# Packed attention and two MoE layers on one core: the first pass of the seven-product layer reordered

## The chip, the cores and the metric

The kernel runs on one core of a Trainium2 chip. TensorE (PE) multiplies, VectorE (DVE), ScalarE (ACT) and GpSimd (POOL) do elementwise work, and SyncE (SP) issues all DMAs of this kernel. Each engine takes its instructions strictly in the order in which they were written, and so does SP's queue: a DMA whose data is not ready holds up every DMA behind it. The metric is the device time of one execution in microseconds (us), the median of several runs.

## The reference, cut to what matters

All arrays are float32 or float64 bits; tokens are 8 batches x 576 = 4608 rows.

```python
p_packed = sm_attn(p, k, v)             # 64 heads, 32 packed rows each
x = sm_attn(q, p_packed, p_packed)      # -> (4608, 512)
h = x @ w_in                            # 512 x 1024
solu = h * softmax(h)
x = layernorm(solu) * g_ln @ w_out      # 1024 x 512
h = x @ moe2_w_in                       # 512 x 2048
g = maximum(h, 0) ** 2
return g @ moe2_w_out                   # 2048 x 512
```

The weights arrive as float64; the kernel reads them as pairs of int32 words and decodes them to float32 itself.

## The kernel before, in words

**Order of the work.** The kernel does not write its instructions directly. It hands operations to a planner (class `Plan`) with an engine, an estimated duration, an urgency (a planned time in us) and the tiles that they read and write. The planner simulates five engines that always take the most urgent operation that is ready, and then writes all instructions in the order that it found. So constants such as `DZ = 6.913` (planned us for one group of the first pass) and the urgency of an operation decide the order on each engine, and nothing else: on the chip only the order and the data count.

**Precision.** Every float32 operand is split into a high part and a rest. `mm` (L389) makes three matmuls of each product: high x high (L396), high x rest (L397), rest x high (L398).

**Stages.** Up to about 536 us the kernel computes attention and the first MoE layer (with POOL's help). Then come two passes for the last two products of the reference, each done with a seven-product scheme on 2 x 2 blocks in place of eight block products.

**First pass** (`z_group`, 536 to 914 us, "z"): `h = x @ moe2_w_in` and `g`. Six blocks of 768 tokens, each with 8 groups. A group has seven products 1, 2, 6, 5, 7, 3, 4 of six matmuls (128 x 128 weights `zi`, 384 columns of `y`), that is 2016 matmuls in all. Products 1, 6, 7 and 4 of a group add up in one bank `px`, one after the other; product 2 goes to `pw`, products 5 and 3 to `pz`. After products 1, 6 and 7 ACT copies the sum so far out of `px` (L928, `snap`), and the next product on `px` must wait for this copy. After product 4 ACT takes the relu (L962). DVE adds `pw` or `pz` to a copy (L932), and DVE (L937) or ACT (L940, L941) takes relu and square of the sum (`finish`). Each result is stored to `g_dram` by a DMA. The copies live in a ring of 11 `gw` slots.

**Weights of the second pass.** While blocks 1 to 4 of the first pass run, 16 calls of `prepare` fetch `moe2_w_out` as raw words (four DMAs of 128 KB into one tile `w2raw`, which the profile shows as `w2raw<-in_moe_w_out_dram` and the order of instructions as `w2raw<-in_moe2_w_out_dram`), decode them (first ACT's absolute value L411, then DVE L414 to L430, whose L430 is the last to read the raw tile), form the seven combinations and store them to `o_dram`. There is one slot for the raw words, `wo20`.

**Second pass** (`o_products`, 914 to 1286 us, "o"): `g @ moe2_w_out`. Six blocks of 768 tokens, seven products 4, 1, 5, 6, 2, 7, 3, each of 8 steps j of nine matmuls (three token tiles, 256 columns), 3024 matmuls in all. Each step needs a 384-column piece `ga` of `g_dram`, split by ACT (L378) and DVE (L381, both write `cb`), and DVE makes sums of pieces (L885). The weights `oi` of a product take over slots of the first pass: those of product 1 two slots of `y` loads (`v01`, `v11`), those of product 4 the four slots of `zi2`. Results are added up in `osb` (L1050, copies L1054) and stored to the output (`store`, L991), four DMAs of 32 rows for each tile of 128 tokens.

Of the kernel before, what the change touches and what calls it, by code (L numbers as in the profile page):

```python
# [245 lines left out]
def kernel(  # L246
# [25 lines left out]
    nc = tc.nc  # L272
# [21 lines left out]
    YB, ZL, OL, GL0, GL1, GL2, PS, CS = 138.73, 119.42, 25.08, 15.29, 10.0, 16.72, -26.16, 142.32  # L294
# [69 lines left out]
    def dma(at, out_, in_, nbytes, r=(), w=()):  # L364
        plan.op(DMA, max(430.0, nbytes / 358.0), at, lambda: nc.sync.dma_start(out=out_(), in_=in_()), r=r, w=w, lag=2200)  # L365
# [406 lines left out]
    def prepare(at, w_bits, rows2, cols2, outs, marks, tiles, r=(), engines=BOTH):  # L772

        raw, x, hi = tiles
        for i, (n, m) in enumerate(((0, 0), (0, 1), (1, 1), (1, 0))):
            dma(at, lambda i=i: raw()[:, i * P:(i + 1) * P], lambda n=n, m=m: w_bits[rows2[n]:rows2[n] + P, 2 * cols2[m]:2 * (cols2[m] + P)].rearrange(
                "p (f w) -> p f w", w=2), P * P * 8, r=list(r), w=[raw])
        decode(at, raw, 4 * P, x, part=lambda t: t[:, :4].rearrange("p b f -> p (b f)"), add=engines)
# [16 lines left out]
    T0, DT = 96.13, 17.76  # L795
    PD0, PD = 168.95, 30.084
    UD, UA, U1 = 32.796, 191.99, -65.87
    WI, WO, WOD, YL = 161.4, 266.68, 57.239, 3.29
# [22 lines left out]
    def weights_z():  # L821
        for k in range(16):
            c, n = divmod(k, 8)
            tiles = [m1.tile([P, 4 * P, 2], I32, "w2raw"), m1.tile([P, 7, P], F32, "wx"),
                     m1.tile([P, 7, P], F32R, "wh", tag="w2raw")]
            prepare(PD0 + PD * k, w2_in_bits, (c * P, (c + 2) * P), (n * P, F2 // 2 + n * P),
                    [lambda k=k, s=s: z_dram[s][:, :, k].rearrange("q p f -> p q f") for s in range(2)], [z_mark], tiles, [under_way])
# [4 lines left out]
    DZ, DO = 6.913, 8.163  # L832
# [24 lines left out]
    def load_o(at, p):  # L857
        def load(t, s, j, w):
            dma(at, lambda: t().bitcast(F32), lambda: o_dram[s][PLACE[p]][:, j:j + w], P * w * 2 * P * 4, r=[o_mark], w=[t])
        if p == 1:  # L860
# [4 lines left out]
        else:  # L865
            q = {7: 1, 4: 2, 5: 6, 6: 5, 2: 7, 3: 3}[p]
# [45 lines left out]

    def z_group(at, st, n):
        bx, bw, bz = pso.tile([P, 512], F32, "px", bufs=4), bank("pw"), bank("pz")
        y = ys[st]

        def product(p, ps, first):
            ts, view = zi[p]

# [4 lines left out]
            plan.op(PE, c_mm(6, HN), at, f, r=ts + y[p], w=[ps])  # L924

        def snap(ps):
            t = gw()
            plan.op(ACT, c_act(HN), at, lambda: nc.scalar.copy(t(), ps()[:, :HN]), r=[ps], w=[t])  # L928
            return t

        def add(t, ps):
            plan.op(DVE, c_dve(HN), at, lambda: nc.vector.tensor_tensor(t(), ps()[:, :HN], t(), op=ALU.add), r=[t, ps], w=[t])  # L932

        def finish(t, b, relu=True):
# [27 lines left out]
        plan.op(ACT, c_act(HN), at, lambda: nc.scalar.activation(c21(), bx()[:, :HN], AF.Relu), r=[bx], w=[c21])  # L962
        finish(c21, 2, False)
# [35 lines left out]
    def o_products(at, st):  # L999
# [13 lines left out]
        x = None  # L1013
        for k, p in enumerate(O_ORDER):
# [5 lines left out]
            for j in range(8):  # L1020
# [3 lines left out]
                if cbs[0] % 6 == 5:  # L1024
# [14 lines left out]
                def f(j=j, ch=ch, cl=cl, acc=acc, wv=wv, first=p not in (6, 7)):  # L1039
                    for i in range(NI):  # L1040
# [36 lines left out]
    def second():  # L1077
# [3 lines left out]
        for st in range(NSZ):  # L1081
            for n in range(8):
                z_group(T1 + DZ * (8 * st + n), st, n)
                k = 8 * st + n - 8
                if 0 <= k < 32 and k % 2 == 0:
                    j, q = divmod(k // 2, 2)
                    tiles = [wo_v.tile([P, 4 * P, 2], I32, "w2raw", tag="wo20"), wo_v.tile([P, 7, P], F32, "wx", tag="wo21"),
                             wo_v.tile([P, 7, P], F32R, "wh", tag="wo30")]
                    prepare(T1 + DZ * (k + 8) + PS, w2_out_bits, (j * P, (j + 8) * P), (q * P, 2 * P + q * P),
                            [lambda j=j, q=q, s=s: o_dram[s][:, :, j, q * P:(q + 1) * P].rearrange("q p f -> p q f") for s in range(2)], [o_mark], tiles, engines=(DVE,))  # L1090
# [41 lines left out]
```

## Time and profile before

| | |
|---|---|
| runs | 1296.13 us median of 3 (1293.94 to 1297.68) |
| the profiled execution | 1294.89 us, its span 1293.1 us |
| mean granted TensorE clock | 0.983 |
| PE matmuls busy | 1228.0 us (95% of the span) |
| PE weight loads busy | 1132.8 us (88%) |
| DVE busy | 945.4 us (73%) |
| ACT busy | 812.0 us (63%) |
| POOL busy | 258.1 us (20%) |

Busy times are sums over the span of one profiled execution; the span runs from the first to the last instruction. PE is shown in two rows, matmuls and weight loads, which overlap. An idle time is put down to what released the instruction behind it. In the rows further down, `L411` is line 411 of the kernel before, `a<-b` says that tile a is written from tile b, and `x17` counts instructions.

### The profile page before, as it was taken

How to read it: one execution, taken by the hardware profiler on the slowest of the kernel's cores; microseconds unless marked ns; L12 is line 12 of the kernel's file. 1: busy time of each engine (PE TensorE's matmuls, PEld its weight loads, DVE VectorE, ACT ScalarE, POOL GpSimd, SP SyncE). 2: the span in 40 equal slices, each digit the busy share in tenths (PEclk: the TensorE clock that was granted, in tenths of full speed). 3: DMA queues.
4: the chain of work that ended last, by engine and by line, in shares of the span. 5: the costliest groups of instructions: out<-in, count | busy, mean ns of one | idle time of the engine just before them, and what ended most of it. 6: DMA issues, size and time to landing. Idle time of an engine off the chain costs nothing.

```text
span 1293.1 us, 23520 instructions
## 1 busy us (share of the span) xinstructions
PE 1228.0 (95%) x8420; PEld 1132.8 (88%) x8420; DVE 945.4 (73%) x1844; ACT 812.0 (63%) x1699; POOL 258.1 (20%) x266
## 2 busy tenths in 40 slices
PE   5878999999999999999999999999899999999997
PEld 3436888887988889999999999999799999999997
DVE  6897888788778865448575868552678797878885
ACT  5666778677777776558676767685455554545452
POOL 2565554456545542000000000000000000000000
PEclk9887999999999999999999999999899999999999
DMA  7652462545354335985657576643985444443501
GB/s 247 207 143 82 124 182 77 154 126 140 107 147 142 102 103 196 324 284 195 212 173 257 167 257 195 213 179 114 362 327 189 124 141 141 124 150 96 176 22 50
DMA packets 176677, 218.10 MB, mean 169 GB/s; under 512 B 22960, under 2 KB 147376, under 8 KB 175792
## 3 DMA queue, kind: packets, MB, share of 16 engines
q1 hardware_dynamic: 176560, 216.60, 53.2%
q8 instruction: 66, 1.08, 0.4%
q14 instruction: 51, 0.42, 0.1%
HBM read 130.55 MB, written 85.98 MB: 167 GB/s over the span
## 4 chain that ended last, share of the span: by engine, by line
PE 66%; DVE 12%; DMA 9%; ACT 6%; issue 3%; SPq 2%; POOL 1%; ACTq 0%; DVEq 0%; POOLq 0%
PE px L396 8%; PE px L397 7%; PE px L398 7%; PE ph L697 6%; PE pa L397 5%; PE pa L398 5%; PE pa L396 5%; PE py L396 4%; PE py L397 4%; PE py L398 4%; DMA w2raw<-in_moe_w_out_dram 3%; SPq L365 2%; PE ptv L740 2%; PE pg L626 1%; PE pz L396 1%
## 5 line engine op out<-in xcount | busy, mean ns | idle before, releaser
L378 ACT CAST cb<-ga 128x384 fp32r<-128x384 f32 x336 | 169.2, 513 | 179.5 <-PE pa L398 75.7
L381 DVE TENSOR_TENSOR cb<-ga,cb 128x384 fp32r<-128x384 f32 x336 | 181.4, 555 | 66.7 <-ACT cb L378 64.0
L396 PE MATMUL py<-v,wo 128*128 128x256 f32 x576 | 167.1, 290 | 0.0
L397 PE MATMUL py<-v,wo 128*128 128x256 f32 x576 | 162.7, 283 | 0.0
L398 PE MATMUL py<-v,wo 128*128 128x256 f32 x576 | 162.7, 283 | 0.0
L398 PE MATMUL px<-oi,cb 128*128 128x256 f32 x504 | 143.8, 285 | 4.1 <-DVE cb L381 4.1
L396 PE MATMUL px<-y,zi 128*128 128x384 f32 x384 | 133.0, 346 | 13.1 <-ACT gw L928 12.7
L396 PE MATMUL px<-oi,cb 128*128 128x256 f32 x504 | 143.0, 284 | 1.1 <-ACT cb L378 1.1
L397 PE MATMUL px<-oi,cb 128*128 128x256 f32 x504 | 143.8, 285 | 0.0
L397 PE MATMUL pa<-oi,cb 128*128 128x256 f32 x504 | 142.6, 283 | 0.0
L398 PE MATMUL pa<-oi,cb 128*128 128x256 f32 x504 | 142.4, 283 | 0.0
L396 PE MATMUL pa<-oi,cb 128*128 128x256 f32 x504 | 141.6, 281 | 0.0
L397 PE MATMUL px<-y,zi 128*128 128x384 f32 x384 | 130.3, 339 | 0.2 <-DVE y L381 0.2
L398 PE MATMUL px<-y,zi 128*128 128x384 f32 x384 | 130.2, 339 | 0.0
L396 PEld LDWEIGHTS py<-v,wo 128*128 128x128 f32 x576 | 110.0, 191 | 3.7 <-issue 2.4
L397 PEld LDWEIGHTS py<-v,wo 128*128 128x128 f32 x576 | 110.2, 191 | 0.7 <-issue 0.2
L398 PEld LDWEIGHTS py<-v,wo 128*128 128x128 f32 x576 | 110.0, 191 | 0.0
L932 DVE TENSOR_TENSOR gw<-pz,gw 128x384 f32<-128x384 f32 x96 | 53.2, 555 | 75.2 <-ACT gw L928 51.6
L885 DVE TENSOR_TENSOR ga<-ga 128x384 f32<-128x384 f32 x192 | 99.8, 552 | 6.4 <-DMA ga<-g_dram 5.5
L398 PEld LDWEIGHTS px<-oi,cb 128*128 128x128 f32 x504 | 96.6, 192 | 4.3 <-DVE cb L381 4.3
L928 ACT COPY gw<-px 128x384 f32<-128x384 f32 x144 | 66.7, 474 | 52.0 <-PE px L398 38.7
L396 PEld LDWEIGHTS px<-oi,cb 128*128 128x128 f32 x504 | 97.4, 193 | 1.3 <-ACT cb L378 1.3
(196 smaller groups left out, 3243.1 us busy)
## 6 DMA issues: line engine op xcount, KB each, us to landing
g_dram<-gw SPq DMA_DIRECT2D x192, 192.0 KB, 2.8
ga<-g_dram SPq DMA_DIRECT2D x96, 384.0 KB, 3.7
zi<-z_dram SPq DMA_DIRECT2D x28, 512.0 KB, 7.1
oi<-o_dram SPq DMA_DIRECT2D x24, 512.0 KB, 9.8
kr<-in_k_dram SPq DMA_DIRECT2D x16, 576.0 KB, 4.5
qr<-in_q_dram SPq DMA_DIRECT2D x16, 576.0 KB, 4.7
y_dram<-ysb SPq DMA_DIRECT2D x72, 128.0 KB, 2.4
yr<-y_dram SPq DMA_DIRECT2D x12, 768.0 KB, 6.6
```

What stands on the lines that cost most here:

```text
L365: plan.op(DMA, max(430.0, nbytes / 358.0), at, lambda: nc.sync.dma_start(out=out_(), in_=in_()), r=r, w=w, lag=2200)
L378: plan.op(ACT, c_act(cols, sbuf=r[0].pool not in (psm, psh, pso)), at, lambda: nc.scalar.copy(out_(), in_()), r=r, w=w)
L381: plan.either(on(cols, *engines), at, lambda e: vec[e].tensor_tensor(out_(), in_(), hi_().bitcast(F32), op=ALU.subtract), r=r, w=w, port=i ...
L396: nc.tensor.matmul(ps, lh, rh, start=first, stop=False, skip_group_check=onto)
L397: nc.tensor.matmul(ps, lh, rl, start=False, stop=False, skip_group_check=onto)
L398: nc.tensor.matmul(ps, ll, rh, start=False, stop=last, skip_group_check=onto)
L626: nc.tensor.matmul(pg()[es, :], ppq()[:, es], wi[2 * g + e]()[:, fs], start=True, stop=True)
L697: nc.tensor.matmul(ph()[:, fs], al[l]()[:, g], g_tiles[b, g]()[:, r, fs], start=ends[0] and g == 0 and t == 0, stop=ends[1] and g == NG - ...
L740: nc.tensor.transpose(pt()[:, c * P:(c + 1) * P], e()[:, (4 * t + c) * P:(4 * t + c + 1) * P], ident)
L885: plan.op(DVE, c_dve(cols), at, lambda: nc.vector.tensor_tensor(out_(), in0(), in1(), op=op), r=r, w=w, port=True)
L928: plan.op(ACT, c_act(HN), at, lambda: nc.scalar.copy(t(), ps()[:, :HN]), r=[ps], w=[t])
L932: plan.op(DVE, c_dve(HN), at, lambda: nc.vector.tensor_tensor(t(), ps()[:, :HN], t(), op=ALU.add), r=[t, ps], w=[t])
```

## The change

1. **Products spread over two groups.** A table `SLOT` gives each product of a group a planned time of its own within two groups' length, so that products of two groups alternate on PE, and the copies, sums and stores behind them have planned times of their own too. Product 7 now comes before 5, and 4 before 3. A mark (`zover`) keeps product 2 of a group behind product 3 of the group two before.
2. **Two slots for raw weights.** `w2raw` alternates between `wo20` and `wo31`; the ring of `gw` copies loses `wo31` and has 10 slots.
3. **Raw loads planned with 3 us to spare** (`LATE`): the planner takes it that they land 3.03 us later, for these loads and for the `yr` loads of blocks 1 to 5. The chip does not wait for this; only the order changes.
4. **First weights of the second pass early.** `oi` of product 4 takes the slots `v01`, `v11`, and those of product 1 the slots of `zi2`.
5. **One store for each output tile**, or two where a tile crosses the end of a batch.
6. **Last product by token tiles.** In the last block, product 3 runs all eight steps for the first tile of 128 tokens, then for the second, then for the third, with eight `cb` slots of its own.
7. Constants of the planner, among them the pace of the first stage (`T0`, `DT`, `PD`, `UD`) and of the first pass (`DZ`). Arguments `sign` that are passed through have the value that was the default.

```diff
-    YB, ZL, OL, GL0, GL1, GL2, PS, CS = 138.73, 119.42, 25.08, 15.29, 10.0, 16.72, -26.16, 142.32
+    SN, FN, LATE = -2.46, 0.61, 3030.11
+    YB, ZL, OL, GL0, GL1, GL2, PS, CS = 198.04, 124.15, 20.73, 15.29, 13.31, 31.48, -5.8, 152.3
...
-    T0, DT = 96.13, 17.76
-    PD0, PD = 168.95, 30.084
+    T0, DT = 64.63, 20.694
+    PD0, PD = 169.1, 27.598
...
-    DZ, DO = 6.913, 8.163
+    DZ, DO = 7.334, 8.163
...
-        plan.op(DMA, max(430.0, nbytes / 358.0), at, lambda: nc.sync.dma_start(out=out_(), in_=in_()), r=r, w=w, lag=2200)
+        plan.op(DMA, max(430.0, nbytes / 358.0), at, lambda: nc.sync.dma_start(out=out_(), in_=in_()), r=r, w=w, lag=2200 + spare)
...
-        if p == 1:
+        if p == 4:
             ts = [wo_v.tile([P, 8, 2 * P], F32R, f"oi{p}{s}", tag=f"v{s}1") for s in range(2)]
...
-            q = {7: 1, 4: 2, 5: 6, 6: 5, 2: 7, 3: 3}[p]
+            q = {7: 1, 1: 2, 5: 6, 6: 5, 2: 7, 3: 3}[p]
...
-    def gw(slots=GW + [(wo_v, f"wo{i}") for i in ("000", "001", "010", "011", "100", "101", "110", "111", "31")]):
+    def gw(slots=GW + [(wo_v, f"wo{i}") for i in ("000", "001", "010", "011", "100", "101", "110", "111")]):
...
+    SLOT = {1: 0, 2: 3, 6: 4, 7: 8, 5: 9, 4: 12, 3: 13}
+    zover = []
...
+        when = lambda p, later=0: at + DZ / 7 * (SLOT[p] + later)
+        over = zover[0] if len(zover) == 2 else None
+        zover.append(plan.mark("zover"))
+        if over:
+            zover.pop(0)
...
-            plan.op(PE, c_mm(6, HN), at, f, r=ts + y[p], w=[ps])
+            plan.op(PE, c_mm(6, HN), when(p), f, r=ts + y[p] + after, w=[ps] + [zover[-1]] * (p == 3))
...
-        product(5, bz, True)
-        product(7, bx, False)
-        c22 = snap(bx)
-        add(c22, bz)
-        finish(c22, 3)
-        product(3, bz, False)
-        add(c12, bz)
-        finish(c12, 1)
+        product(7, bx, False)
+        c22 = snap(7, bx)
+        product(5, bz, True)
+        add(5, c22, bz)
+        finish(5, c22, 3)
         product(4, bx, False)
...
+        product(3, bz, False)
+        add(3, c12, bz)
+        finish(3, c12, 1)
...
-        for n in range(P // T):
+        n = 0
+        while n < P // T:
             b, blk = divmod(tok // T + n, NB)
+            w = min(NB - blk, P // T - n)
...
+            n += w
...
-                plan.op(PE, c_mm(3 * NI, H), uj, f, r=cb + [wt(0, j), wt(1, j), chain], w=acc + [chain])
+                if tail:
+                    last.append((f, cb + [wt(0, j), wt(1, j)]))
...
+            for i in range(NI):
+                for f, r in last:
+                    plan.op(PE, c_mm(3, H), u + DO / NI * i, lambda f=f, i=i: f([i]), r=r + [chain], w=[acc[i], chain])
...
-                    tiles = [wo_v.tile([P, 4 * P, 2], I32, "w2raw", tag="wo20"), wo_v.tile([P, 7, P], F32, "wx", tag="wo21"),
+                    tiles = [wo_v.tile([P, 4 * P, 2], I32, "w2raw", tag=("wo20", "wo31")[k // 2 % 2]), wo_v.tile([P, 7, P], F32, "wx", tag="wo21"),
```

The lines of the changed kernel are numbered 3 higher in its first part (L411 becomes L414, L885 becomes L888) and 16 higher from `z_group` on (L928 becomes L944, L932 L948, L940 and L941 L956 and L957, L962 L975).

**Place 1: one set of raw weights, block 1 of the first pass.** SP's rows before, at the fifth of the 16 sets; the number behind a name is that of its buffer, and `g_dram12_101` is result 2 of block 1.

```order
L365 DMA w2raw_7469<-in_moe2_w_out_dram 128x256
L365 DMA g_dram11_100<-gw_7395 128x384
L365 DMA o_dram0_93<-wh_7483 128x7x128
L365 DMA o_dram1_94<-wx_7413 128x7x128
L365 DMA w2raw_7469<-in_moe2_w_out_dram 128x256
L365 DMA g_dram13_102<-gw_7502 128x384
L365 DMA g_dram10_99<-gw_7491 128x384
L365 DMA g_dram12_101<-gw_7523 128x384
L365 DMA w2raw_7469<-in_moe2_w_out_dram 128x256 x2
L365 DMA g_dram11_100<-gw_7471 128x384
```
In the same place of ACT's rows before, the absolute value that reads `w2raw_7469` is the last but one.

```order
L941 ACTIVATE gw_7502<-gw_7502 128x384
L962 ACTIVATE gw_7523<-px_7398 128x384
L941 ACTIVATE gw_7523<-gw_7523 128x384
L940 ACTIVATE gw_7471<-gw_7471 128x384
L941 ACTIVATE gw_7471<-gw_7471 128x384
L928 COPY gw_7547<-px_7473 128x384
L928 COPY gw_7563<-px_7550 128x384
L411 ACTIVATE wx_7565<-w2raw_7469 128x512
L928 COPY gw_7574<-px_7473 128x384
```
The last two of the four raw loads stand behind the store of `gw_7523`, which ACT finishes in the third of these rows; five rows further on ACT reads the raw words. Over the 16 sets this distance, from the last row of ACT that a store ahead of the last raw load waits for to the absolute value, is 6, 11, 15, 5, 5, 8, 16, 9, 9, 8, 13, 8, 9, 8, 13 and 8 rows.

SP's rows of the change around the sixth set, `w2raw_7470`:

```order
L368 DMA w2raw_7470<-in_moe2_w_out_dram 128x256
L368 DMA g_dram12_101<-gw_7466 128x384
L368 DMA g_dram11_100<-gw_7379 128x384
L368 DMA o_dram0_93<-wh_7494 128x7x128
L368 DMA o_dram1_94<-wx_7424 128x7x128
L368 DMA g_dram13_102<-gw_7503 128x384
L368 DMA g_dram10_99<-gw_7491 128x384
L368 DMA w2raw_7470<-in_moe2_w_out_dram 128x256 x3
```
ACT's rows of the change that lead to the absolute value of this set:

```order
L944 COPY gw_7614<-px_7547 128x384
L381 CAST wh_7623<-wx_7556 128x896
L975 ACTIVATE gw_7625<-px_7472 128x384
L957 ACTIVATE gw_7625<-gw_7625 128x384
L944 COPY gw_7645<-px_7629 128x384
L944 COPY gw_7656<-px_7547 128x384
L956 ACTIVATE gw_7656<-gw_7656 128x384
L957 ACTIVATE gw_7656<-gw_7656 128x384
L956 ACTIVATE gw_7645<-gw_7645 128x384
L957 ACTIVATE gw_7645<-gw_7645 128x384
L944 COPY gw_7688<-px_7629 128x384
L414 ACTIVATE wx_7691<-w2raw_7470 128x512
```
The last three loads now stand behind the stores of `gw_7503` and `gw_7491`; ACT finishes `gw_7503` eleven rows ahead of the first row shown, so that 22 rows lie between. Over the 16 sets the distance is 11, 79, 13, 46, 21, 22, 50, 46, 21, 22, 50, 46, 21, 22, 50 and 46 rows.

**Place 2: from the first pass to the second.** SP's rows before, where `oi4..` are weights of product 4 of the second pass and `g_dram02`, `g_dram03` results 2 and 3 of block 0:

```order
L365 DMA g_dram53_118<-gw_10270 128x384
L365 DMA g_dram50_115<-gw_10259 128x384
L365 DMA g_dram52_117<-gw_10293 128x384
L365 DMA oi410_10321<-o_dram1_94 128x1024
L365 DMA g_dram51_116<-gw_10243 128x384
L365 DMA oi401_10332<-o_dram0_93 128x1024
L365 DMA oi411_10343<-o_dram1_94 128x1024
L365 DMA g_dram53_118<-gw_10334 128x384
L365 DMA g_dram52_117<-gw_10353 128x384
L365 DMA ga_10373<-g_dram02_97 128x768
L365 DMA g_dram51_116<-gw_10323 128x384
L365 DMA ga_10376<-g_dram02_97 128x768
```
SP's rows of the change in the same place:

```order
L368 DMA ga_10267<-g_dram03_98 128x768
L368 DMA g_dram51_116<-gw_10171 128x384
L368 DMA ga_10281<-g_dram03_98 128x768
L368 DMA oi700_10293<-o_dram0_93 128x1024
L368 DMA g_dram53_118<-gw_10278 128x384
L368 DMA g_dram50_115<-gw_10269 128x384
L368 DMA ga_10324<-g_dram03_98 128x768
L368 DMA ga_10343<-g_dram03_98 128x768
L368 DMA g_dram52_117<-gw_10326 128x384
L368 DMA g_dram51_116<-gw_10238 128x384
L368 DMA ga_10364<-g_dram02_97 128x768
L368 DMA ga_10373<-g_dram02_97 128x768
```
The weights of product 4 no longer stand between the last stores of the first pass (they are loaded well before), and both first loads of `g_dram02` stand together behind the stores of `gw_10326` and `gw_10238`. DVE's rows before:

```order
L932 TENSOR_TENSOR gw_10243<-pz_10236,gw_10243 128x384
L381 TENSOR_TENSOR cb_10307<-ga_10272,cb_10307 128x384
L932 TENSOR_TENSOR gw_10334<-pz_10311,gw_10334 128x384
L932 TENSOR_TENSOR gw_10323<-pz_10311,gw_10323 128x384
L885 TENSOR_TENSOR ga_10261<-ga_10373,ga_10261 128x384
L381 TENSOR_TENSOR cb_10383<-ga_10261,cb_10383 128x384
L885 TENSOR_TENSOR ga_10272<-ga_10376,ga_10272 128x384
```
DVE's rows of the change:

```order
L953 SCALAR_TENSOR_TENSOR gw_10362<-gw_10362 128x384
L384 TENSOR_TENSOR cb_10375<-ga_10343,cb_10375 128x384
L953 SCALAR_TENSOR_TENSOR gw_10385<-gw_10385 128x384
L384 TENSOR_TENSOR cb_10388<-ga_10324,cb_10388 128x384
L948 TENSOR_TENSOR gw_10313<-pz_10355,gw_10313 128x384
L888 TENSOR_TENSOR ga_10267<-ga_10364,ga_10267 128x384
L888 TENSOR_TENSOR ga_10281<-ga_10373,ga_10281 128x384
L384 TENSOR_TENSOR cb_10402<-ga_10267,cb_10402 128x384
```
Before, one sum (L885 on `ga_10373`, a piece of `g_dram02`) stands ahead of the split of step j = 1 (`cb_10383`); in the change two sums stand ahead of it (L888 on `ga_10364` and `ga_10373`, then L384 on `cb_10402`). On PE the first product of the second pass began behind the last product of the first pass; in the change its step j = 0 stands ahead of the last group's products 7, 5, 4 and 3, and its step j = 1 behind them.

**Place 3: the end.** SP's last rows before (`osb` is an output tile; 32x512 stands for 32 rows of 512 columns):

```order
L365 DMA out_0_dram<-osb_14692 32x512 x4
L365 DMA out_0_dram<-osb_14695 32x512 x4
L365 DMA out_0_dram<-osb_14803 32x256 x4
L365 DMA out_0_dram<-osb_14805 32x256 x4
L365 DMA out_0_dram<-osb_14808 32x256 x4
```
The last rows of the change:

```order
L368 DMA out_0_dram<-osb_14576 4x32x512
L368 DMA out_0_dram<-osb_14579 4x32x512
L368 DMA out_0_dram<-osb_14687 4x32x256
L368 DMA out_0_dram<-osb_14689 2x32x256 x2
L368 DMA out_0_dram<-osb_14692 4x32x256
```
Twelve stores of the last product become four; the middle tile crosses the end of a batch and has two.

## Rows read from the trace of the kernel before

**Rows 1.** Windows: us, busy us (count) by engine, PE's clock, DMA share, GB/s.

```profile
120.00:536.00 416.00, 414.11 (x3005) 365.85 (x3006) 310.29 (x573) 291.42 (x628) 201.14 (x215) 1.00 0.48 145
536.00:914.40 378.40, 364.22 (x2033) 354.12 (x2033) 240.95 (x476) 259.09 (x543) 0.00 (x0) 0.99 0.64 209
914.40:1285.70 371.30, 366.07 (x3025) 365.47 (x3024) 293.56 (x616) 185.32 (x391) 0.00 (x0) 0.99 0.49 157
1285.70:1293.10 7.40, 0.02 (x1) 0.00 (x0) 0.48 (x2) 0.00 (x0) 0.00 (x0) 0.73 0.20 53
```

**Rows 2.** Windows within the first pass, and the undisturbed part of the second.

```profile
536.00:620.00 84.00, 80.68 (x455) 77.58 (x455) 55.99 (x112) 58.29 (x126) 0.00 (x0) 1.00 0.75 251
620.00:830.00 210.00, 200.17 (x1106) 194.16 (x1105) 149.59 (x296) 142.51 (x294) 0.00 (x0) 0.98 0.66 209
830.00:908.00 78.00, 78.00 (x449) 77.64 (x448) 33.53 (x65) 54.76 (x116) 0.00 (x0) 1.00 0.45 158
875.00:905.00 30.00, 30.00 (x175) 30.00 (x173) 8.74 (x16) 17.87 (x37) 0.00 (x0) 1.00 0.32 111
...
930.00:1285.00 355.00, 355.00 (x2962) 355.00 (x2961) 284.37 (x597) 179.40 (x379) 0.00 (x0) 1.00 0.47 148
```

**Rows 3.** Waits, 536 to 914.5 us: us in total, times, longest.

```profile
PEld px L396 <- ACT gw L928: 20.2, 24, 2.3
...
ACT wx L411 <- DMA w2raw<-in_moe_w_out_dram: 15.4, 11, 2.5
...
ACT gw L928 <- DMA g_dram<-gw: 7.7, 3, 3.1
```

**Rows 4.** Timeline around 625 us: start, duration, instruction, idle before it and releaser.

```profile
624.05 0.34 PE L398 MATMUL pw<-y,zi 128*128 128x384 f32 x1
624.97 0.66 ACT L411 ACTIVATE wx<-w2raw 128x512 f32<-128x512 f32 x1 [2.15 <-DMA w2raw<-in_moe_w_out_dram]
625.53 0.46 ACT L928 COPY gw<-px 128x384 f32<-128x384 f32 x1
...
626.05 0.44 PE L396 MATMUL px<-y,zi 128*128 128x384 f32 x1 [1.66 <-ACT gw L928]
```

**Rows 5.** SP's own waits, 536 to 914.5 us.

```profile
SPq L365 <- ACT gw L941: 140.8, 82, 6.2
```

**Rows 6.** Windows with a lowered TensorE clock.

```profile
710.00:720.00 10.00, 8.42 (x39) 8.42 (x40) 7.19 (x14) 5.51 (x11) 0.00 (x0) 0.83 0.31 100
921.00:927.00 6.00, 5.62 (x26) 5.62 (x27) 4.27 (x9) 1.89 (x4) 0.00 (x0) 0.50 1.03 396
```

**Rows 7.** Waits, 536 to 914.5 us: ACT's other wait in the first pass.

```profile
ACT gw L940 <- DVE gw L932: 34.3, 56, 1.4
```

**Rows 8.** Timeline, 910 to 922 us.

```profile
910.34 0.44 PE L396 MATMUL px<-y,zi 128*128 128x384 f32 x1 [0.46 <-ACT gw L928]
...
915.25 0.44 SPq L365 DMA_DIRECT2D ga<-g_dram  x1
...
916.73 0.39 PE L396 MATMUL px<-oi,cb 128*128 128x256 f32 x1 [1.08 <-ACT cb L378]
...
920.30 0.56 DVE L885 TENSOR_TENSOR ga<-ga 128x384 f32<-128x384 f32 x1 [5.13 <-DMA ga<-g_dram]
...
921.38 0.58 PE L398 MATMUL px<-oi,cb 128*128 128x256 f32 x1 [4.15 <-DVE cb L381]
```

**Rows 9.** Timeline, the last 8 us.

```profile
1285.04 1.14 DVE L1050 TENSOR_TENSOR osb<-osb,pa 128x256 f32<-128x256 f32 x3 [4.50 <-PE pa L398]
...
1285.44 0.28 PE L398 MATMUL pa<-oi,cb 128*128 128x256 f32 x1
1285.49 5.42 SPq L365 DMA_DIRECT2D out_dram<-osb  x12
```

**Rows 10.** DMA issues: count, KB each, median us from issue to landing.

```profile
g_dram<-gw SPq DMA_DIRECT2D x192, 192.0 KB, 2.8
ga<-g_dram SPq DMA_DIRECT2D x96, 384.0 KB, 3.7
...
y_dram<-ysb SPq DMA_DIRECT2D x72, 128.0 KB, 2.4
...
out_dram<-osb SPq DMA_DIRECT2D x144, 32.0 KB, 1.6
```

More of the change, by code (lines that the diff above doesn't have):

```diff
@@ L293 @@
     SUB, KLO, ALO = (POOL,), (POOL,), (POOL,)
[L294 removed]
+    ZSIN, OSIN = DVE, DVE
+    SN, FN, LATE = -2.46, 0.61, 3030.11
+    YB, ZL, OL, GL0, GL1, GL2, PS, CS = 198.04, 124.15, 20.73, 15.29, 13.31, 31.48, -5.8, 152.3
     NST = NT // ST
@@ L770, with prepare @@
     PLACE = {1: 0, 4: 1, 3: 2, 2: 3, 5: 4, 7: 5, 6: 6}
-    def prepare(at, w_bits, rows2, cols2, outs, marks, tiles, r=(), engines=BOTH):
+    def prepare(at, w_bits, rows2, cols2, outs, marks, tiles, sign, r=(), engines=BOTH, spare=0):
         raw, x, hi = tiles
@@ L826, in weights_z @@
             prepare(PD0 + PD * k, w2_in_bits, (c * P, (c + 2) * P), (n * P, F2 // 2 + n * P),
-                    [lambda k=k, s=s: z_dram[s][:, :, k].rearrange("q p f -> p q f") for s in range(2)], [z_mark], tiles, [under_way])
+                    [lambda k=k, s=s: z_dram[s][:, :, k].rearrange("q p f -> p q f") for s in range(2)], [z_mark], tiles, ZSIN, [under_way])
     weights_z()
     ORDER = (1, 2, 6, 5, 7, 3, 4)
-    DZ, DO = 6.913, 8.163
+    DZ, DO = 7.334, 8.163
     T1 = T0 + DT * NT / P
@@ L915, in z_group @@
         y = ys[st]
+        when = lambda p, later=0: at + DZ / 7 * (SLOT[p] + later)
[3 more added lines that the diff above has]
+            zover.pop(0)
         def product(p, ps, first):
             ts, view = zi[p]
+            after = [over] if over and p == 2 else []
             def f():
@@ L1011, in banks @@
             return [bank("pa") for _ in range(NI)]
-        x = None
+        x, last = None, []
         for k, p in enumerate(O_ORDER):
@@ L1023, in o_products @@
                 sv = lambda t=t, at_=at_: t()[:, at_]
-                if cbs[0] % 6 == 5:
+                tail = st == NSZ - 1 and k == len(O_ORDER) - 1
+                if tail:
+                    cb = [w2i.tile([P, 2, HN], F32R, "cb", tag=f"zi{(2, 6)[j // 4]}{j // 2 % 2}{j % 2}")]
+                    ch, cl = (lambda o=o, t=cb[0]: t()[:, o] for o in range(2))
+                elif cbs[0] % 6 == 5:
                     cb = [m2.tile([P, HN], F32R, "cb", tag=f"gw{i}") for i in range(2)]
@@ L1037, in o_products, with f @@
                 wv, wt = oi[p]
-                def f(j=j, ch=ch, cl=cl, acc=acc, wv=wv, first=p not in (6, 7)):
-                    for i in range(NI):
+                def f(tiles, j=j, ch=ch, cl=cl, acc=acc, wv=wv, first=p not in (6, 7)):
+                    for i in tiles:
                         ts = slice(i * P, (i + 1) * P)
                         mm(acc[i]()[:, :H], (ch()[:, ts], cl()[:, ts]), [wv(s, j)[1] for s in range(2)], j == 0 and first, j == 7, not first)
-                plan.op(PE, c_mm(3 * NI, H), uj, f, r=cb + [wt(0, j), wt(1, j), chain], w=acc + [chain])
+                if tail:
+                    last.append((f, cb + [wt(0, j), wt(1, j)]))
+                else:
+                    plan.op(PE, c_mm(3 * NI, H), uj, lambda f=f: f(range(NI)), r=cb + [wt(0, j), wt(1, j), chain], w=acc + [chain])
+            for i in range(NI):
+                for f, r in last:
+                    plan.op(PE, c_mm(3, H), u + DO / NI * i, lambda f=f, i=i: f([i]), r=r + [chain], w=[acc[i], chain])
             u += DO
```

48 lines of the change are left out of this document (24 added, 24 removed).

## The prediction

> **What bounds the kernel now.** I read the windows by stage first. From 120 to 536 us PE stands still for 1.9 us [rows 1]; no engine order can give much there. The first pass shows 14.2 us without a matmul (378.40 less 364.22), the second 5.2, and behind the last matmul 7.4 us pass.
>
> Idle time understates what is lost, since matmuls overlap and a stretched one counts as busy. So I take the spacing at full speed and count: 30.00 us hold 173 weight loads, 0.1734 us for each 384-column matmul; 355.00 us hold 2962 matmuls of the second pass, 0.1199 us each [rows 2]. The first pass has 2033 matmuls, 2016 of its own and 17 of 256 columns left over from the first stage: 2016 x 0.1734 + 17 x 0.12 = 351.6 us. It takes 378.4, so **26.8 us are lost**. By stretches: 536 to 620 us 84.0 - (438 x 0.1734 + 2.0) = 6.0; 620 to 830 us 210 - 1106 x 0.1734 = 18.2; 830 to 908 us 78 - 449 x 0.1734 = 0.1 [rows 2]; the rest in the last 6 us. The loss thus sits where weights are prepared and is absent where none are, with the same products on PE. The Trainium skill ("Perfetto Trace Analysis", section Identifying the Most-Contended Engine) calls matmul busy time a bad measure of TensorE and points to the busy share of weight loads: these leave 24.3 us here, nearer to my 26.8 than to 14.2. By 24.3 the forecast would be some 2.5 us later; the spacing is what the sum uses.
>
> The waits name the cause. PE's weight loads wait 20.2 us for ACT's copy L928; ACT's absolute value L411 waits 15.4 us for raw words, 11 times [rows 3]. One case in full: the last matmul on `pw` starts at 624.05, ACT stands 2.15 us at L411 for its DMA, starts it at 624.97, and only then copies `px` at 625.53; the next matmul starts at 626.05 [rows 4]. At 0.17 spacing it was due at 624.22: 1.83 us lost because the copy is queued behind an absolute value whose words are late. The words are late because SP waits 140.8 us for squares by ACT (L941) in front of stores [rows 5], and the loads stand behind these. Place 1 of the orders shows it: of the 16 sets 11 have nine ACT rows or fewer between such a square and the absolute value, and there are 11 waits. PE pays twice: after some stops its clock goes to 1.2 GHz for part of a stretch (0.83 over 10 us, 1.7 us lost [rows 6]).
>
> **The change, part by part.**
>
> *Raw loads and slots, and products over two groups: the first pass.* The shortest distance becomes 11 rows, most are 21 to 79. Sets with 11 or more did not wait before, so I expect no wait at L414 and none of its copies late. The new product order puts three other products (3 x 1.04 = 3.1 us) between two on the same bank, where before one or two lay; a copy of 0.46 us [rows 4] and its way fit into that. What remains: the start, 536 to 620 us, has 6.0 lost now, partly from late first weights; I leave 3.5 (1 to 6). In 620 to 830 us a pass without the 15.4 us could be as good as 830 to 908 us (0.1/78, so 0.3 for 210); but ACT and DVE are busy 68 and 71% there against 70 and 43% in the later stretch [rows 2], and ACT also waits 34.3 us for DVE in front of squares [rows 7], which can still hold up a copy. I take 3 of 18.2 left (0.3 to 10), nearer to the clean stretch because its ACT share is the same. With 0.8 for the end, 7.3 us stay lost: **gain 26.8 - 7.3 = 19.5, taken as 19** for a clock dip or two that I cannot place.
>
> *Transition.* The second pass loses 371.30 - 3025 x 0.1199 = 8.6 us, nearly all at its start: PE stops 1.08 us at 916.73 and 4.15 at 921.38, then runs 6 us at 0.50 of its clock [rows 6, 8]. Before, block 2 of `g_dram` was asked for at 915.25, 4.9 us after the last product 7 began (910.34), and DVE had it at 920.30, 5.05 later [rows 8]. In the change the `oi4` loads are out of the way, so the load follows product 7 by some 1.6 us (its 1.04 us and a hop). But only products 7, 5, 4 and 3 (4.2 us) now cover it, since step j = 0 has moved ahead of them, and two sums stand ahead of the split (place 2). With T the start of that product 7: issue T + 1.6, second piece 0.44 later, landing 3.7 (median [rows 10]) to 5.05, two sums and a split at 0.5 to 0.56 each: split ready at T + 6.9 to T + 8.3, PE at T + 4.2. A stop of 2.7 to 4.1 us stays, and with it half clock of 1.7 to 2.9 (the two stretches [rows 6]; the second has 26 matmuls in 6.0 us, 3.1 at full speed). Loss 5.5 in the middle, ends 2 and 9: **gain 3.1** (-0.4 to 6.6). What is late next is product 1's weights, needed 8.6 us after the first; I give that nothing, since they follow the pieces in the queue and 512 KB land in the cover of a whole product.
>
> *Tail.* The last matmul starts at 1285.44; SP issues 12 stores for 5.42 us [rows 9], 0.45 each; the last, issued at 1290.46, lands 1.6 us later [rows 10], and the span ends 1.0 behind. By tiles, the first two tiles' sums and stores lie under the third's 24 matmuls (2.9 us), which is longer than their 3 issues. Behind it come one sum, which as the third of three ended 0.74 us after that matmul's start (1286.18 [rows 9]), one store of 128 KB, 2.4 from issue to landing [rows 10], and the 1.0: 1285.44 + 0.74 + 2.4 + 1.0 = 1289.6 against 1293.1, **gain 3.5** (2.7 if it lands like the 2.8 of `g_dram`, up to 4.3 if like 1.6). Stores merged earlier cost nothing: SP does not bind the second pass.
>
> *First stage.* Up to some 190 us all engines keep their order; beyond, attention units come earlier and first-layer weights every 27.6 in place of 30.1 us. PE is full there, and the work is the same: **0**, by bounds 3 either way.
>
> **Sum:** 19 + 3.1 + 3.5 = 25.6 us. The profiled execution took 1294.89, so 1269.3; it lies 1.2 below the median, so the forecast is **1270** (likeliest case alone: 1261 to 1276).
>
> **Rivals.**
>
> (a) *Half the first pass's loss stays.* The absolute value was only the most visible stop; ACT's 34.3 us behind DVE [rows 7], or late `y` tiles at block starts, hold up copies as soon as it goes. For it: ACT and DVE are both near 70%. Against: the clean stretch with ACT at 70%. Price: 10 us in 620 to 830 in place of 3, the start unchanged at 6: 1270 + 7 + 2.5, about 1280.
>
> (b) *The first stage loses.* More changes between kinds of work or a gap of ACT in the new order cost 3% of the 346 us from 190 on, 10 us: 1280. Against: as many changes between kinds on PE (295, before 299).
>
> (c) *Slower: the ring of copies is too short.* Ten slots in place of 11, and `c12` now lives from product 6 to product 3 of the same group, 9 x 1.04 = 9.4 us, then a sum, square, SP's wait and landing. A slot comes round after some 22 us; a life of 9.4 + 1.7 + SP's wait (up to 6.2 [rows 5]) + landing (2.8 to 6) is 14 to 23 us. ACT already waits for a store to land three times, 7.7 us [rows 3]. If 2.6 us of this fall on PE in one group of four (12 of 48), 31 us are lost and the time is 1301; from 10 groups on the change gains nothing. The Trainium skill ("Perfetto Trace Analysis", section Optimization Strategy) says that a bubble that repeats can mean too few buffers, which speaks for this; the trace has three such waits, not a repeating one.
>
> (d) *The raw words stay late*, because SP waits longer than the planner thinks. Only transition and tail gain: 1270 + 19, 1289.
>
> **How the numbers follow.** Chances: forecast 0.66, (a) 0.17, (b) 0.07, (c) 0.06, (d) 0.04. The range reaches from 1261 (start at its lower bound, 2.5; 620 to 830 at 0.3, 2.7 more; transition at its better end, 3.5) through (a) and (b) with 4 us above: **1261 to 1284**, which leaves out (c), (d) and the outermost of the first. About 0.3% (4 us) is what a measurement can tell from no change: faster 0.91 (all but (c) and some of (d)), the same 0.03, slower 0.06.
>
> **What would show it.** Right: no wait of L414 for raw words; PE's waits for L944 under 3 us in all; clock 1.00 from 620 to 830 us; a stop of 2.7 to 4.1 us in the second pass's first product; one sum and one store behind the last matmul and a span ending 3.9 us behind it. Wrong: waits L944 for `g_dram` stores (c), repeated PE idle behind L948 or L956 (a), PE idle between 190 and 536 us (b).

## The result, and the profile after

The changed kernel took **1279.43 us** (1278.16 to 1280.6, 4 runs) beside 1296.20 of the kernel before on the same chip, a ratio of 0.9872 (95% interval 0.9855 to 0.9889): 16.8 us faster. The forecast was 1270, its range 1261 to 1284, the likeliest case alone 1261 to 1276: the time lies in the range and outside the likeliest case. The profiled execution has a span of 1276.4 us, 16.7 less than before.

The windows by stage of the changed kernel (us, busy us and count of PE, PEld, DVE, ACT, POOL, PE's clock, DMA share, GB/s; the stages now end at 897.3 and 1266.6) answer to [rows 1]:

```profile
120.00:536.00 416.00, 412.31 (x2991) 364.62 (x2988) 311.75 (x576) 293.73 (x628) 202.21 (x214) 1.00 0.49 152
536.00:897.30 361.30, 358.97 (x2057) 354.60 (x2055) 227.85 (x449) 273.91 (x582) 0.00 (x0) 1.00 0.66 211
897.30:1266.60 369.30, 364.76 (x3016) 364.32 (x3015) 293.44 (x617) 183.66 (x391) 0.00 (x0) 0.99 0.48 157
1266.60:1276.40 9.80, 0.18 (x2) 0.00 (x0) 0.42 (x1) 0.00 (x0) 0.00 (x0) 0.78 0.19 68
```

The first pass is 17 us shorter. The stretch behind the last matmul has grown from 7.4 to 9.8 us; counted from that matmul's start it was to shrink from 7.7 to 3.9 us and is 9.9. Within the first pass, the window that answers to [rows 2] has PE's clock at 1.00 in place of 0.98:

```profile
620.00:830.00 210.00, 208.46 (x1187) 205.55 (x1186) 147.01 (x289) 161.63 (x342) 0.00 (x0) 1.00 0.69 216
```

The waits between 536 and 897 us answer to [rows 3, 7]:

```profile
ACT gw L956 <- DVE gw L948: 58.0, 69, 2.1
...
ACT wx L414 <- DMA o_dram<-wx: 8.7, 9, 1.5
...
PEld px L399 <- ACT gw L944: 5.0, 10, 0.9
...
PE px L399 <- ACT gw L944: 2.1, 5, 0.6
...
ACT gw L944 <- DMA g_dram<-gw: 1.6, 1, 1.6
```

L414 no longer waits for raw words at all; what it still waits for is its own tile `wx`, which a store to `o_dram` must have read. The wait of PE's weight loads (PEld) for copies fell from 20.2 us to 5.0. ACT waits longer for DVE than before (58.0 against 34.3) although PE waits less for ACT.

The timeline at the start of the second pass and at the end:

```profile
901.03 0.58 PE L399 MATMUL px<-oi,cb 128*128 128x256 f32 x1 [3.60 <-ACT cb L381]
...
912.53 0.39 PE L400 MATMUL pa<-oi,cb 128*128 128x256 f32 x1 [0.93 <-DMA oi<-o_dram]
...
1261.57 6.76 SPq L368 DMA_DIRECT2D out_dram<-osb  x4
...
1266.50 0.28 PE L401 MATMUL pa<-oi,cb 128*128 128x256 f32 x1
...
1266.81 0.42 DVE L1080 TENSOR_TENSOR osb<-osb,pa 128x256 f32<-128x256 f32 x1 [2.42 <-PE pa L401]
```

The last sum ends at 1267.23, 0.73 behind the last matmul's start, close to the 0.74 of the prediction; SP has issued its last store by 1268.4. The span ends at 1276.4. So 8 us pass in which no engine works and the transfers run out. The windows of this stretch show how:

```profile
1263.00:1267.00 4.00, 3.78 (x32) 3.57 (x31) 0.61 (x2) 0.00 (x0) 0.00 (x0) 1.00 0.26 102
1267.00:1271.00 4.00, 0.00 (x0) 0.00 (x0) 0.23 (x1) 0.00 (x0) 0.00 (x0) 1.00 0.26 99
```

A share of 0.26 of the 16 DMA engines is the work of about four, at 100 GB/s together, for eight us on end.

### The profile page after: what moved, and what is told of

Its sections match the earlier page's. It is cut to its first block, busy times and chain, and to the rows that moved or that the text cites. A ratio compares the mean times of both kernels' runs of the same rounds, so it can differ in the third digit from the quotient of the medians.

```text
span 1276.4 us, 23378 instructions
## 1 busy us (share of the span) xinstructions
PE 1220.6 (96%) x8420; PEld 1131.8 (89%) x8420; DVE 934.3 (73%) x1821; ACT 827.9 (65%) x1738; POOL 259.5 (20%) x265
## 4 chain that ended last, share of the span: by engine, by line
PE 73%; DVE 9%; ACT 6%; DMA 6%; issue 3%; POOL 1%; SPq 1%; ACTq 0%; DVEq 0%; POOLq 0%
PE px L399 9%; PE px L400 9%; PE px L401 9%; PE ph L700 6%; PE pa L400 5%; PE pa L401 5%; PE pa L399 5%; PE py L399 3%; PE py L400 3%; PE py L401 3%; PE pz L401 2%; PE pz L399 2%; PE pz L400 2%; PE ptv L743 2%; ACT y L381 1%
## 5 line engine op out<-in xcount | busy, mean ns | idle before, releaser
L384 DVE TENSOR_TENSOR cb<-ga,cb 128x384 fp32r<-128x384 f32 x336 | 180.7, 554 | 66.4 <-ACT cb L381 64.7
L948 DVE TENSOR_TENSOR gw<-pz,gw 128x384 f32<-128x384 f32 x96 | 53.2, 554 | 81.0 <-PE pz L401 70.7
L888 DVE TENSOR_TENSOR ga<-ga 128x384 f32<-128x384 f32 x192 | 99.6, 551 | 3.1 <-DMA ga<-g_dram 2.3
L956 ACT ACTIVATE gw<-gw 128x384 f32<-128x384 f32 x113 | 59.2, 524 | 59.5 <-DVE gw L948 59.2
```

Source lines behind the costliest of these rows:

```text
L384: plan.either(on(cols, *engines), at, lambda e: vec[e].tensor_tensor(out_(), in_(), hi_().bitcast(F32), op=ALU.subtract), r=r, w=w, port=i ...
L888: plan.op(DVE, c_dve(cols), at, lambda: nc.vector.tensor_tensor(out_(), in0(), in1(), op=op), r=r, w=w, port=True)
L948: plan.op(DVE, c_dve(HN), when(p, SN), lambda: nc.vector.tensor_tensor(t(), ps()[:, :HN], t(), op=ALU.add), r=[t, ps], w=[t])
L956: nc.scalar.activation(t(), t(), AF.Relu)
```

## The experiments

All have one way of counting, that of the prediction. *First stage*: the first matmul of the first pass, plus 0.12 us for each matmul of the first stage that comes behind it. *First pass* and *second pass*: their length less 0.1734 or 0.1199 us for each matmul in it, that is what they lose against full speed. *End*: from the last matmul's start to the end of the span. The four make up the differences of the spans. Each row is one execution.

| profiled execution | first stage done | first pass loses | second loses | end | span |
|---|---|---|---|---|---|
| before | 537.9 | 27.0 | 8.6 | 7.7 | 1293.1 |
| changed | 539.6 | 7.1 | 7.9 | 9.9 | 1276.4 |
| changed again (e0) | 544.1 | 6.9 | 5.8 | 9.9 | 1278.9 |
| e1 four stores | 545.4 | 8.4 | 7.3 | 5.7 | 1278.8 |
| e2 pairs | 541.6 | 6.9 | 7.4 | 21.2 | 1289.1 |
| e3 before, raw slots | 537.5 | 17.5 | 8.5 | 7.7 | 1283.2 |
| e4 one raw slot | 542.9 | 19.0 | 6.5 | 9.9 | 1290.4 |
| e5 old first stage | 540.9 | 14.1 | 6.1 | 9.9 | 1283.1 |
| e6 old `oi` slots | 541.6 | 10.7 | 12.7 | 9.9 | 1286.9 |
| e7 sums behind pair | 542.5 | 6.7 | 8.9 | 9.9 | 1280.0 |
| e9 sums, two queues | 544.3 | 8.4 | 10.5 | 5.0 | 1280.2 |
| e10 two queues | 541.7 | 6.2 | 6.8 | 3.9 | 1270.5 |
| e11 old first stage, mixed | 536.1 | 19.4 | 7.6 | 3.9 | 1279.1 |

**The changed kernel again (e0)**, a control for e5, e7 and e9 on their chip.

> The changed kernel itself, beside the next three on one chip. Theory A (its own order of the first stage costs some 4 us) and rival B (the later starts of the first pass seen in some of the runs above, 3 to 6 us, are scatter between executions and chips): 1277 to 1281 by both. By A the first pass starts, with the matmuls of the first stage that are left over counted, 2 to 6 us later than in the kernel before; by B on average as early.

1281.91 us, ratio 0.9892 (0.9874 to 0.9910), 14.0 us under the kernel before on this chip. Its first stage ends 6.2 us later than that of the kernel before: A's side, just over its 2 to 6.

**The end: four stores, and pairs.** e1 puts the four stores of 32 rows back; e2 cuts the last block's merged stores in two.

```diff
-            w = min(NB - blk, P // T - n)
+            w = min(NB - blk, P // T - n, 2 if tok >= (NSZ - 1) * 2 * HN else P // T)
```

> The changed kernel with four stores of 32 rows for each output tile again, everything else as changed. Theory A (a merged store, whose outermost dimension is 4 or 2 blocks of 32 rows, runs on only 4 or 2 of the 16 DMA engines, so that the 1.2 MB of the last two products leave at some 100 GB/s and the span ends 9.9 us behind the last matmul): the last tile's four stores end some 4.7 us behind the last matmul's start (0.74 for the sum, 3 x 0.45 for issues, 1.6 landing, 1.0 end), DMA share above 0.3 while they run; 1274, 5 us under the changed kernel. Rival B (the bytes of products 7 and 3 simply come too close together in any form, or the order by tiles is to blame): the end stays 9 to 10 us behind the last matmul, 1278 to 1281.

> The changed kernel with its stores of the last block only cut into pairs (64 KB or 128 KB for two blocks of 32 rows), twice as many DMAs, all else as changed. Theory A (outermost dimension 2: two of 16 DMA engines, share 0.125, some 50 GB/s): products 7 and 3 leave 1.18 MB in some 24 us from 1262 on, the span ends about 1286, time about 1289, 10 us over the changed kernel. Rival B (size of a DMA or issue time sets the end): smaller DMAs end no later, 1276 to 1281.

e1: 1277.57 us, ratio 0.9852 (0.9829 to 0.9876), its end 5.7 us. e2: 1291.05 us, 0.9964 (0.9948 to 0.9980), its end 21.2 us. The last block's stores carry the same bytes in all three. The windows of e1 while the stores of product 7 and then the last ones of product 3 leave:

```profile
1266.00:1268.00 2.00, 2.00 (x19) 2.00 (x18) 0.54 (x2) 0.00 (x0) 0.00 (x0) 1.00 0.50 126
...
1274.00:1276.00 2.00, 0.00 (x0) 0.00 (x0) 0.00 (x0) 0.00 (x0) 0.00 (x0) 1.00 0.27 70
```

and of e2 behind its last matmul (1267.93):

```profile
1270.00:1276.00 6.00, 0.00 (x0) 0.00 (x0) 0.00 (x0) 0.00 (x0) 0.00 (x0) 0.63 0.13 51
1276.00:1282.00 6.00, 0.00 (x0) 0.00 (x0) 0.00 (x0) 0.00 (x0) 0.00 (x0) 0.50 0.13 50
```

0.13 of 16 is two engines, at 50 GB/s. A store of two blocks of 32 rows takes the share of two engines, one of four blocks that of four, though more stores stand issued behind it; whether these wait for the same engines or for the store ahead, the share does not tell. Theory A holds: what the number of blocks sets is the rate, about 25 GB/s for each block. The Trainium skill ("DMA: Bandwidth & Descriptors", section Rules for kernel authors) says it outright: an outermost dimension smaller than 16 confines a DMA to at most that many engines. The traces agree: 0.13 with two, 0.26 with four, 0.50 with 32 rows outermost. It is the end that decides here, not e1's time, which lies between A's 1274 and B's 1278; the execution profiled, whose first stage ended latest of all, took 1280.62. The share of e1's last stores, 0.27, is under the 0.3 that A expected, and its end is 1 us longer; its timeline shows SP issuing stores until 1276.62, 3.5 us behind the last matmul:

```profile
1258.84 17.78 SPq L368 DMA_DIRECT2D out_dram<-osb  x36
```

**The first pass: raw slots alone, product order alone.** e3 gives the kernel before the two slots and the spare time; e4 takes them from the changed one, with the spare time of its `yr` loads.

```diff
-                    tiles = [wo_v.tile([P, 4 * P, 2], I32, "w2raw", tag="wo20"), ...
+                    tiles = [wo_v.tile([P, 4 * P, 2], I32, "w2raw", tag=("wo20", "wo31")[k // 2 % 2]), ...
```

> The kernel before with two slots for raw words, the ring of copies cut to 10 slots, and these loads planned with 3 us to spare; product order, first stage, transition and stores as before. The rows of ACT between a square that a store ahead of the last raw load waits for and the absolute value become 11 to 47. Theory A (late raw words cause the first pass's loss): no wait of L411 for raw words, 14 to 19 of the 26.8 us lost come back, 1278 to 1282. Rival B (the order of products on the banks causes it: a copy has only one or two products' time): 2 to 6 us come back, 1290 to 1294.

> The changed kernel with one slot for raw words, 11 slots for copies and no spare time for raw and y loads; product order over two groups stays. Nine of 16 sets have 9 ACT rows or fewer ahead of the absolute value, so it waits for raw words again in about nine sets. Theory A (late raw words alone): 9 x 1.4 us of ACT's waits and their clock dips come back on PE, 10 to 15 us, 1290 to 1294. Rival B (three products between two of one bank absorb a late copy): ACT waits some 12 us, PE loses under 4, 1280 to 1284.

e3: 1285.32 us, 0.9915 (0.9895 to 0.9934). e4: 1294.77 us, 0.9989 (0.9975 to 1.0003). The waits of e3 in the first pass:

```profile
ACT gw L941 <- DVE gw L933: 43.7, 65, 2.1
...
PEld px L397 <- ACT gw L929: 10.9, 19, 1.5
...
ACT wx L412 <- DMA w2raw<-in_moe_w_out_dram: 0.8, 1, 0.8
```

and of e4:

```profile
ACT wx L414 <- DMA w2raw<-in_moe_w_out_dram: 12.4, 9, 2.6
PEld px L399 <- ACT gw L944: 11.7, 18, 1.9
```

In e3 the wait for raw words is gone (0.8 us of 15.4) and 9.5 of 27.0 us come back; 17.5 stay lost, with PE's weight loads still waiting 10.9 us for copies. ACT's longest wait there is for DVE, in front of squares; what held up each copy was not followed. In e4 the words are late in nine sets, as the orders said, and 12 us are lost again, so its rival B, that three products between two on one bank absorb a late copy, fails. Neither theory has it alone: raw slots with their spare time give 9.5 in the old order of products and 12 in the new; everything else that was changed, the order of products and the constants, gives 8.0 with late words and 10.4 without.

One caution holds for all runs of the first pass: the planner plans each kernel anew, and an edit moves rows that it does not name. Matched in sequence from the traces, some 60% of ACT's rows of the first pass stand in e3 as in the kernel before, and some 30% in e4 as in e0; over 99% stand as in e0 in e6 and e10.

**The first stage: its old constants.** e5 puts `QA` to `UN`, `WDS`, `WIS`, `T0`, `DT`, `PD0`, `PD`, `UD` to `U1`, `WI` and `WOD` back; e12 gives the changed ones to the kernel before.

```diff
...
-    T0, DT = 64.63, 20.694
-    PD0, PD = 169.1, 27.598
...
+    T0, DT = 96.13, 17.76
+    PD0, PD = 168.95, 30.084
...
```

> The changed kernel with the planner's constants of the first stage as before (pace of attention units, of the first MoE layer and of its weights), first and second pass as changed. Theory A (the new order of the first stage costs some 4 us): the first pass starts 3 to 5 us earlier, 1275 to 1277. Rival B (the order there costs nothing): 1278 to 1281, as the changed kernel beside it.

> The kernel before with the changed kernel's constants of the first stage alone. Theory A (that order costs 4 us): PE stands still for 5 to 7 us from 120 to 536 in place of 1 to 2; the first three sets of raw words have more room and give some 3 us back, 1295 to 1299. Rival B (the order costs nothing): idle 1 to 3 us, 1291 to 1294.

e5: 1282.07 us, 0.9897 (0.9879 to 0.9915), as e0 beside it, and just over B's 1278 to 1281. The windows of e0:

```profile
120.00:536.00 416.00, 409.73 (x2967) 361.70 (x2967) 310.22 (x572) 294.46 (x630) 202.96 (x215) 1.00 0.48 148
```

and of e5:

```profile
120.00:536.00 416.00, 412.76 (x2996) 364.41 (x2995) 309.16 (x571) 292.56 (x630) 202.12 (x216) 1.00 0.47 143
```

PE stands still for 6.3 us in e0, 3.2 in e5 and 1.9 before; the other kernels with the changed order of the first stage have 3.7 to 7.5. So A is right about this stage, whose end comes 3.2 us earlier. But e5's first pass loses 14.1 in place of 6.9, 6.2 of these 7.2 us more in its first two blocks, and the time is the same. So the small loss of the changed kernel's first pass hangs on these constants too. e5 does not undo the first stage alone: ACT's rows of the first pass match those of e0 to some 87%, and the first pass starts 74 us earlier in the plan. e12 took 1296.76, 0.9998 (0.9985 to 1.0012), in A's range; but A expects there a loss and a gain that nearly cancel, and no trace of an execution of that length was kept that could tell them from nothing. This one settles nothing.

**The transition: old slots, and sums behind a pair.** e6 gives product 4 the slots of `zi2` again; e7 writes DVE's sums of steps j and j + 1 behind both splits.

```diff
...
-                    add_sub(uj + later, view(d), view(i0), view(i1), op, [raw[i0][j][0], raw[i1][j][0]], [raw[d][j][0]], HN)
+                    sums.append((uj + later, view(d), view(i0), view(i1), op, [raw[i0][j][0], raw[i1][j][0]], [raw[d][j][0]], HN))
+                if j % 2:
+                    for a in sums:
+                        add_sub(*a)
+                    sums.clear()
...
```

> The changed kernel with the weights of product 4 of the second pass in the slots of zi2 again and those of product 1 in the two slots of y loads, so that product 4 begins behind the whole first pass. Theory A (loading product 4's weights early is what took the second pass's loss from 8.6 to about 7 us): the second pass loses 8 to 10 us, its time 1 to 3 us over the changed kernel, 1281 to 1284. Rival B (only block 2's pieces, which wait for product 7's slots, set the start): it loses 6 to 8 as in the changed kernel, 1279 to 1282.

> The changed kernel, but VectorE's sums of two steps j are written behind the splits of both steps, so that the first product of the second pass no longer has the sum with block 2 of the first results between its steps 0 and 1. Theory A (the stop of 3.6 us at its start and the half clock of 2.4 us behind it hang on this sum alone): no stop above 1 us there, 5 us less, 1273 to 1275. Rival B (what is late next, the pieces of block 0 or the weights of product 1 of the second pass, which PE already waited 0.9 us for, takes its place): a stop of 2 to 3 us some 9 us later, 1277 to 1280.

e6: 1286.07 us, 0.9918 (0.9900 to 0.9936); its second pass loses 12.7 and its first 10.7, more than A expected. e7: 1282.15 us, 0.9899 (0.9882 to 0.9915), as e0 (1281.91). e7's timeline is nearer to rival B:

```profile
904.65 0.39 PE L399 MATMUL px<-oi,cb 128*128 128x256 f32 x1 [1.37 <-ACT cb L381]
...
906.85 0.39 PE L401 MATMUL px<-oi,cb 128*128 128x256 f32 x1 [1.70 <-DVE cb L384]
...
910.13 0.58 PE L401 MATMUL px<-oi,cb 128*128 128x256 f32 x1 [1.44 <-DVE cb L384]
```

In e0 there were two:

```profile
904.49 0.39 PE L399 MATMUL px<-oi,cb 128*128 128x256 f32 x1 [2.60 <-ACT cb L381]
...
905.69 0.58 PE L401 MATMUL px<-oi,cb 128*128 128x256 f32 x1 [0.69 <-DVE cb L384]
```

Two stops became three, on other pieces, 4.5 us together in place of 3.3.

**A better end.** e9 has e7's sums, four stores for each tile, and half of the last product's twelve stores on ScalarE's queue; e10 has the four stores too, no change of the sums, and every second of the last 24 stores there.

```diff
...
+            act = tok >= (NSZ - 1) * 2 * HN and (c0 or c1 - c0 > 2 * P) and n % 2
...
+            if act:
+                plan.op(ACT, 100.0, at - 100, lambda o=o, i_=i_: nc.scalar.dma_start(out=o(), in_=i_()), r=[t], lag=2200)
...
```

These lines are e10's; in e9 the condition `act` picks fewer stores.

> The changed kernel with sums behind the pair as above, four stores for each output tile (16 DMA engines each), and of the last product's twelve stores six issued by ScalarE in place of SyncE. Theory A (with four stores SyncE's own queue set the end, 12 issues of product 7 and 12 of product 3 at 0.45 to 0.49 us): the span ends 3.5 to 4.5 us behind the last matmul's start, 5.5 to 6.5 us less than with one store, and 5 less by the sums: 1267 to 1270. Rival B (landing, not issuing, sets the end): the end stays 5.5 us behind the last matmul, 1270 to 1273.

> The changed kernel with four stores for each output tile, and in the last block every second store issued by ScalarE in place of SyncE; sums as changed. Theory A (with one store per tile few DMA engines set the end, with four SyncE's issuing): the span ends 4 to 5 us behind the last matmul's start in place of 9.9, 5 to 6 us less, 1274 to 1276. Rival B (the end gained is lost in stalls before it, since 12 stores per product stand in the queue of the pieces): stalls in the second pass of 3 us or more, 1278 to 1281.

e9: 1280.91 us, 0.9881 (0.9863 to 0.9898), above both ranges: its end is 5.0, but its second pass loses 10.5, with stops as in e7. **e10: 1272.47 us, 0.9819 (0.9798 to 0.9839)**, the fastest kernel here; its interval lies below both that the changed kernel had against the kernel before. Its end:

```profile
1266.62 0.28 PE L401 MATMUL pa<-oi,cb 128*128 128x256 f32 x1
...
1266.93 0.42 DVE L1082 TENSOR_TENSOR osb<-osb,pa 128x256 f32<-128x256 f32 x1 [2.43 <-PE pa L401]
1267.38 0.78 SPq L368 DMA_DIRECT2D out_dram<-osb  x2
1267.39 0.85 ACTq L1014 DMA_DIRECT2D out_dram<-osb  x2
```

The span ends at 1270.5, 3.9 us behind the last matmul's start, what the prediction had given to the change itself.

**The first stage in e10 as before, its planned gap to the first pass as changed (e11).**

```diff
...
-    T1 = T0 + DT * NT / P
+    T1 = T0 + DT * NT / P + 74.11
...
```

> The kernel of the two queues with the first stage's constants as before, but the planned start of the first pass where the change has it, which leaves a later planned time between the stages. Theory A (the first stage's own order costs 4 us in waits of PE for the results of the first MoE layer and for VectorE): PE stands still for under 4 us from 120 to 536 in place of 5 to 7, 1271 to 1273 if the first pass keeps its 7 us of loss. Rival B (the first pass's first blocks pay it back, as with the first stage's constants alone): a loss of 11 to 15 us in the first pass, 1276 to 1280.

1283.93 us, 0.9901 (0.9883 to 0.9919), above both ranges. The first stage ends at 536.1, the earliest of all, and the first pass loses 19.4, not in its first blocks alone but in all but the last. PE's weight loads wait for copies again, and not behind raw words:

```profile
PEld px L399 <- ACT gw L944: 11.3, 18, 1.6
...
ACT wx L414 <- DMA w2raw<-in_moe_w_out_dram: 1.3, 1, 1.3
```

The loss is rival B's and larger, but its place is another. Again the rest did not stay as it was: ACT's rows of the first pass match those of e10 to some 54%. So neither e5 nor e11 shows what the first stage costs with the first pass held fixed. They do show that the table `SLOT` and two raw slots by themselves don't bring a loss of 7 us.

## Why the prediction was right, and where not

**First pass: right in size, half right in cause.** 19 us were forecast, 27.0 - 7.1 = 19.9 came. No wait for raw words and a clock of 1.00 from 620 to 830 us were foretold and came; so did PE's wait for L944 of under 3 us, if the matmuls' 2.1 is meant and not the weight loads' 5.0, which is the row that the prediction reads before the change. But the chain from the late word to the late copy explains only 9.5 us by itself (e3). The other 10.4 came with the rest of the change. The prediction named one part of it, the new order of products, in a sentence ("fit into that"); that the 3.1 us between two uses of a bank are what carries it is not shown. With the same table `SLOT` and ACT waiting for raw words only 2.5 us (e5) and 1.3 us (e11), the first pass lost 14.1 and 19.4 us under other constants, and PE's weight loads waited 11.3 us for copies in e11. So the gain needs the whole order that the planner found, and which of its features counts stays open.

**Transition: right mechanism, gain too large.** A stop of 2.7 to 4.1 us with half clock behind it was forecast and is there: 3.60, then 27 matmuls at 0.21 us. The second pass loses 7.9 in place of 5.5. The step that failed is "I give that nothing" for product 1's weights: PE waits 0.93 us for them, which is part of the 2.4 us. The rest is not traced to a term; in the other runs of the same order here (e0, e1, e2, e4, e10) the loss is 5.8 to 7.4, with a first stop of 2.6 us, a second of 0.5 to 1.7, and a wait for these weights of 0.88 us at most. That the early weights matter is shown by e6, which loses 12.7 without them.

**Tail: the wrong sign.** Forecast +3.5 us, measured -2.2. The step that failed is "one store of 128 KB, 2.4 from issue to landing", priced from the row of `y_dram` [rows 10]: the same bytes, but not the same shape, since that one lists 128 rows outermost and this one four blocks of 32. At four engines the 1.18 MB of products 7 and 3 need 11.6 us at 102 GB/s, from about 1262 on, whatever the last sum does. So "Stores merged earlier cost nothing" fails with it: the stores of product 7 are still leaving when those of product 3 are issued. e2 doubles that time, e1 and e10 take it away.

**First stage: not zero.** "PE is full there, and the work is the same: 0" holds for the work, not for the order: PE stands still for 3.7 to 7.5 us in place of 1.9, and the stage ends 1.7 us later in the profiled execution, up to 7.5 in others. This is rival (b), at a fifth to three quarters of its price. With the old constants PE stands still for 0.6 to 3.2 us (before, e3, e5, e11), so the longer stand goes with the new ones and is not scatter alone. Undoing them gave 3.2 and 5.6 us back there, and the first pass, planned anew, lost 7.2 and 13.2 more (e5 against e0, e11 against e10); why was not found.

**Sum.** -1.7 + 19.9 + 0.7 - 2.2 = 16.7, the difference of the spans; forecast 0 + 19 + 3.1 + 3.5 = 25.6. Of the 8.9 us between, the tail has 5.7, the transition 2.4 and the first stage 1.7, less 0.9 from the first pass. The range held by its width, which is luck: rivals (a) and (b) had stretched it to 1284, and neither is what brought the time there. (a) did not occur, (b) did in small part, (c) not (one wait of 1.6 us for a slot), nor (d). The largest part of the miss, the tail, was in no rival.

## What to carry to other kernels

Price a DMA by a row of the same shape, not of the same size: merging small stores into one whose outermost dimension is the number of blocks saves issues and takes engines away, which shows as a DMA share of that number in 16, and it costs most where nothing is left to hide it. Where several parts of a change serve one wait, test each alone and both together: here the loads on time brought 9.5 us by themselves, all else 8.0, and both 19.9. Where a planner orders everything anew, compare the orders too before a difference is put down to the edit: a part that looks foreign to a stage can move it. A stage at 99% can still lose several us to a new order, and undoing it can cost the next stage more than it gives back.

## What the hardware showed that was not expected

Merged stores of 1 or 2 KB rows ran at some 25 GB/s for each block of their outermost dimension: 50 GB/s and a share of 0.13 with two, 100 and 0.26 with four. SP issues a store of 32 rows in 0.39 to 0.49 us, ScalarE in 0.43 (two in 0.85), side by side in e10, so that the last four stores are issued in the time of two. The changed first stage, in the same order, ended between 539.6 and 545.4 us in nine executions, a scatter that the spans carry on.
